# State of a head pair as one block-diagonal matrix, multiplied on the whole TensorE array

## Chip, cores and metric

One core of a Trainium2 chip. The metric is device microseconds (us) of one execution, the median of repeated runs. A span is the time from the first to the last instruction of one profiled execution, which is a little shorter than that execution's own time.

## Reference

Three layers follow each other. B = 2 batches, H = 8 heads, S = 768 positions, D = 64 features per head, so 512 features in all.

```
for t in range(S):                       # retention, gamma differs by head
    state = gamma[None, :, None, None] * state + einsum('bhd,bhe->bhde', k[:, :, t], v[:, :, t])
    y[:, :, t] = scale * einsum('bhd,bhde->bhe', q[:, :, t], state)
x = y.transpose(0, 2, 1, 3).reshape(B, S, 512)

h = (x.transpose(0, 2, 1) @ U @ V)       # U 768x32, V 32x768
u = x + h.transpose(0, 2, 1)
x = u + relu(u @ w_ch1) @ w_ch2          # 512 -> 2048 -> 512

h = relu(x @ w_in)                       # 512 -> 1024
u, v = halves of h
v_n = layer norm of v over its 512 features
v_s = einsum('ts,bsd->btd', w_spatial, v_n) + b_spatial
return (u * v_s) @ w_out                 # 512 -> 512
```

Inputs q, k, v and the biases are 32-bit floats; the weights of U, V, w_ch1, w_ch2, w_in and w_out are 64-bit and are turned into 32-bit on the chip.

## The kernel before

**Retention in chunks.** Heads are taken in pairs, i = 0..7 (four pairs per batch). A pair fills the 128 partitions: head e of the pair has partitions 64e to 64e+63. The 768 positions are cut into six chunks of 128. For each pair the work on TensorE is:

- `scores` (tile `sc`): q times k within each chunk, one matrix of 128x128 for each head and chunk. VectorE, or ScalarE and GpSimd, scale and mask it into `pt` (L418 to L421).
- also in `scores`, L424 to L429 (tile `ds`): what each of the first five chunks adds to the state, k transposed times v, 64x64 for each head. k has been scaled by ScalarE before (`kk`, L395). Then one VectorE scan (L431) runs over the chunks and gives `s`, the state before each of the chunks 1 to 5: 64 features of a head in its own 64 partitions, and along the free axis 64 columns times five chunks, the chunk being the fastest index. So the 64 values of a chunk lie five elements apart.
- `mix` (tile `x`): for each half h of the positions (three chunks), `intra` adds v times `pt` (L450), and `inter` adds state times q for chunks 1 to 5 (L444). The result goes through VectorE into the matrix `X` (L453).
- `turn` (tile `t`, L469) transposes X, `down` (tile `g`) multiplies by U, `up` (tile `hu`) by V.

**Shapes on the array.** The matmuls of these stages use different parts of the 128x128 array, and the plan gives each operation a word for it: "keys" for `scores` (64 rows, 128 columns), "tokens" for `ds` and `intra` (128 rows, 64 columns), "state" for `inter` (64 rows, 64 columns, one head in the upper left quarter and one in the lower right), and False for everything on the whole array: `t`, `g`, `hu` and all later layers. A matmul of 32-bit floats stands as two records (two loads of weights, two matmuls) in the trace; `inter` has 8 pairs x 5 chunks x 2 heads x 2 = 160 of them.

**Order of the work.** No order is written out. Each operation is given to a planner (`Plan`) with a key (roughly a due time), the engines that may do it, a cost in ns, the buffers that it reads and writes, and its word for the array. `arrange` walks forward in modelled time and always gives out the operation that can start first on its engine, by key among those that can start at once. On TensorE an operation whose word differs from that of the one before it is held to start 130 ns later (`span`, L133). `latest` walks backward for the latest end that each operation may have, and `settle` repeats both, ROUNDS times, moving each key towards that latest time by the share BLEND. So the order on all engines, over the whole kernel, comes from the planner's costs, from ROUNDS and from BLEND. Where the planner sees TensorE empty for over 500 ns in the first 60 us, it fills in matmuls whose result nobody reads (tile `idle`). Where an operation may run on VectorE or GpSimd, the planner chooses.

**Buffers.** Pool "a" has 36 slots of 128 x 768 floats and holds q, k, kk, v, `pt`, transposed X and the operands of the later layers. Pool "s" has two slots and holds `s`. A slot is free again when the planner's last reader has ended. All big loads are issued from SyncE.

**After retention.** The channel layer (`c`, `acc`, and `q...`, products in the manner of Strassen) starts on batch 0 while the last pairs of batch 1 are still in retention; then come the gate layer, the spatial product (`pz`) and the output product (`o`). The channel layer's `acc` alone is 768 matmuls of 128x128 by 384 columns.

Of the kernel before, what the change touches and what calls it, by code (L numbers as in the profile page):

```python
# [8 lines left out]
F32 = mybir.dt.float32  # L9
# [12 lines left out]
P = 128  # L22
# [21 lines left out]
class Plan:  # L44
# [16 lines left out]
    def op(self, eng, fn, r=(), w=(), key=None, size=0):  # L61

        o = Op()
        o.key, o.eng, o.fn, o.size = (self.key if key is None else key), dict(eng), fn, size
        deps, bufs = {}, []
        for tok in list(r) + list(w):
            b = tok if isinstance(tok, Buf) else tok[0]
            if isinstance(b, Buf) and b not in bufs:
                bufs.append(b)
                b.left += 1  # L70
        for tok in r:
            if tok in self.last:
                deps[self.last[tok].seq] = self.last[tok]
        for tok in w:
            for x in self.readers.get(tok, ()):
                deps[x.seq] = x
            if tok in self.last:
                deps[self.last[tok].seq] = self.last[tok]
        for tok in w:
            self.last[tok] = o  # L80
            self.readers[tok] = []
        for tok in r:
            if tok not in w:
                self.readers.setdefault(tok, []).append(o)
        o.deps = list(deps.values())
        o.key = max([o.key] + [x.key + 1e-6 for x in o.deps])
        o.bufs, o.outs, o.need, o.seq = bufs, [], len(o.deps), len(self.ops)
        for d in o.deps:
            d.outs.append(o)
        self.ops.append(o)  # L90
        return o
# [206 lines left out]
BIAS = {'V': 0.0, 'G': 0.0, 'A': -200.0}  # L298
HARM = 10.0
NEAR = 5.0  # L300
ROUNDS, BLEND = 14, 0.5
WARM = 11
FILL = 60000.0
AT0, AT1, CH0, CH1 = 6.0, 28.0, 45.0, 15.0
# [18 lines left out]
def tile_kernel(ctx: ExitStack, tc: tile.TileContext, a, out: bass.AP):  # L323
# [10 lines left out]
    def mm(o, l, r, start, stop):  # L334
        nc.tensor.matmul(o, l, r, start=start, stop=stop, skip_group_check=True)  # L335
# [4 lines left out]
    def dma(dst, src, size, r=(), w=(), key=None, eng="D"):  # L340
        op({eng: (55.0, False)}, lambda e: e.dma_start(dst(), src()), r, w, key, size)

    sc_t = const.tile([P, 2 * H + NP * (NCH - 1)], F32, name="scales")
    ksc, msc = sc_t[:, 0:H], sc_t[:, H:2 * H]
    shared = Buf("a", [P, NP + 2, P], F32, "shared")
    GS, TRI, IDENT = [(shared, p) for p in range(NP)], (shared, NP), (shared, NP + 1)

# [50 lines left out]
    def scores(i):  # L398
        b, p = divmod(i, NP)
        for e in range(2):  # L400
            pt_t[i, e] = Buf("a", [P, NCH, P], F32, f"pt{i}{e}")
        for h in range(2):
            sc = [bank([P, TC, P], f"sc{i}{e}{h}") for e in range(2)]

            def run(_, h=h, sc=sc):
                for c in range(TC):
                    sl = slice((TC * h + c) * P, (TC * h + c + 1) * P)
                    for e in range(2):
                        r = slice(64 * e, 64 * e + 64)
                        mm(sc[e].t[:, c, :], k_t[i].t[r, sl], q_t[i].t[r, sl], True, True)  # L410
            op({"P": (690, "keys")}, run, r=[(k_t[i], h), (q_t[i], h)], w=sc)
            for e in range(2):
                m = msc[:, 2 * p + e:2 * p + e + 1]

                def pt(e=e, h=h):
                    return pt_t[i, e].t[:, TC * h:TC * h + TC, :]
                if (2 * h + e) in VIA[i]:
                    op({"A": (582, False)}, lambda E, pt=pt, x=sc[e], m=m: E.activation(pt(), x.t, AF.Copy, scale=m), r=[sc[e], "sc"], w=[(pt_t[i, e], h)])  # L418
                    op({"G": gss(T)}, lambda E, pt=pt: E.tensor_mul(pt(), pt(), tri()), r=[(pt_t[i, e], h), TRI], w=[(pt_t[i, e], h)])
                else:  # L420
                    op({"V": (611, False)}, lambda E, pt=pt, x=sc[e], m=m: E.scalar_tensor_tensor(pt(), x.t, m, tri(), ALU.mult, ALU.mult), r=[sc[e], "sc", TRI], w=[(pt_t[i, e], h)])  # L421
        ds = bank([P, D, NCH - 1], f"ds{i}")

        def run(_):  # L424
            for c in range(NCH - 1):
                for e in range(2):
                    r = slice(64 * e, 64 * e + 64)
                    mm(ds.t[r, :, c], kk_t[i].t[:, c, r], v_t[i].t[:, c, r], True, True)
        op({"P": (600, "tokens")}, run, r=[(kk_t[i], 0), (kk_t[i], 1), v_t[i]], w=[ds])  # L429
        s_t[i] = s = Buf("s", [P, D * (NCH - 1)], F32, f"s{i}")  # L430
        op({"V": (830, False)}, lambda E: E.tensor_tensor_scan(s.t, decay[p // 2].t[:, p % 2, :], ds.t.rearrange("p d c -> p (d c)"), 0.0, ALU.mult, ALU.add), r=[ds, (decay[p // 2], p % 2)], w=[s])  # L431

    def mix(i):
        b, p = divmod(i, NP)
        for h in range(2):
            x = bank([P, TC, P], f"x{i}{h}")
            cs = range(TC * h, TC * h + TC)
            c0 = max(1, TC * h)

            def inter(_, x=x, cs=cs, c0=c0, h=h):  # L440
                for c in cs[c0 - TC * h:]:
                    for e in range(2):
                        r = slice(64 * e, 64 * e + 64)
                        mm(x.t[r, c - TC * h, :], s_t[i].t[r, :].rearrange("p (d c) -> p d c", c=NCH - 1)[:, :, c - 1], q_t[i].t[r, c * P:(c + 1) * P], False, True)  # L444

            def intra(_, x=x, cs=cs, h=h):
                for c in cs:
                    for e in range(2):
                        r = slice(64 * e, 64 * e + 64)
                        mm(x.t[r, c - TC * h, :], v_t[i].t[:, c, r], pt_t[i, e].t[:, c, :], c == cs[0], False)  # L450
            op({"P": (656, "tokens")}, intra, r=[v_t[i], (pt_t[i, 0], h), (pt_t[i, 1], h)], w=[x])
            op({"P": (440 if h == 0 else 655, "state")}, inter, r=[s_t[i], (q_t[i], h)], w=[x])
            op({"V": vps(T)}, lambda E, x=x, h=h: E.tensor_mul(xs(b, p, h).rearrange("p (c t) -> p c t", t=P), x.t, gs(p).unsqueeze(1).to_broadcast([P, TC, P])), r=[x, GS[p]], w=[("X", b, p, h)])  # L453

    def cpy(e, o, i):
# [262 lines left out]
    A = {}  # L718
# [133 lines left out]
    with tc.manual_schedule():  # L852
# [8 lines left out]
            op({"P": (n * 320.0, False)}, lambda _: spend(n), w=[idle])  # L861

        plan.key = -200.0
        dma(lambda: sc_t[:], lambda: a["sc"], P * 36 * 4, w=["sc"], eng="E")
        op({"G": (250.0, False)}, lambda e: e.memset(shared.t[:, NP:NP + 2, :], 1.0), w=[TRI, IDENT])
        for z, (tok, test) in enumerate(((TRI, ALU.is_ge), (IDENT, ALU.is_equal))):
            op({"G": (400.0, False)}, lambda e, z=z, test=test: e.affine_select(shared.t[:, NP + z, :], shared.t[:, NP + z, :], [[1, P]], test, 0.0, base=0, channel_multiplier=-1), r=[tok], w=[tok])
# [98 lines left out]
def _arrays(q, k, v, moe_U, moe_V, moe_w_ch1, moe_w_ch2, moe2_w_in, moe2_w_spatial, moe2_b_spatial, moe2_w_out):  # L966
    import numpy as np

    def c(x):
        return np.ascontiguousarray(x)  # L970

    def featmaj(x):
        return c(x.transpose(0, 1, 3, 2).reshape(B, NP, P, S))

    def tokmaj(x):
        return c(x.reshape(B, NP, 2, NCH, P, D).transpose(0, 1, 4, 3, 2, 5).reshape(B, NP, P, NCH, P))

    gamma = 1.0 - 2.0 ** (-5.0 - np.arange(H, dtype=np.float64))
    t = np.arange(P, dtype=np.float64)
    scale = 1.0 / np.sqrt(D)  # L980
    gs = np.repeat(gamma[:, None] ** t[None, :] * scale, D, axis=0).reshape(NP, P, P)
    ksc = gamma[None, :] ** (P - t[:, None])
    msc = gamma[None, :] ** -t[:, None]
    gc = np.repeat(gamma ** P, D).reshape(NP, P).T
    gc = np.concatenate([np.zeros((P, NP, 1)), np.repeat(gc[:, :, None], NCH - 2, axis=2)], axis=2).reshape(P, NP * (NCH - 1))

    def f32(x):
        return c(x.astype(np.float32))

    def raw(x):  # L990
        return c(x).view(np.uint64)

    def ftiles(x):
        n = x.shape[1] // P
        return raw(x.reshape(ND, P, n, P).transpose(2, 1, 0, 3).reshape(n, P, DM))

    def halves(x):
        return raw(x.reshape(2, 2, P, 2, 2 * P).transpose(1, 3, 2, 0, 4).reshape(ND, P, DM))

    return {  # L1000
        "qT": featmaj(q), "kT": featmaj(k), "k": tokmaj(k), "v": tokmaj(v),
        "gs": f32(gs.transpose(1, 0, 2)), "sc": f32(np.concatenate([ksc, msc, gc], axis=1)),
        "U": raw(moe_U.reshape(NCH, P, R).transpose(1, 0, 2).reshape(P, NCH * R)), "V": raw(np.tile(moe_V, (4, 1)).reshape(P, 2, T).transpose(1, 0, 2)),
        "w1": ftiles(moe_w_ch1),
        "w2": raw(moe_w_ch2.reshape(NF, P, DM)),
        "wu": ftiles(moe2_w_in[:, :DM]), "wv": halves(moe2_w_in[:, DM:]),
        "ws": f32(moe2_w_spatial.T.reshape(NCH, P, S)),
        "bsp": c(moe2_b_spatial.reshape(1, S)),
        "wo": raw(moe2_w_out.reshape(ND, P, DM)),
    }  # L1010
# [17 lines left out]
```

## Time and profile before

| | |
|---|---|
| median of 3 runs | 464.26 us (464.25 to 464.81) |
| the profiled execution: own time | 464.74 us |
| its span | 463.0 us |
| TensorE busy | 457.6 us (99% of the span) |
| VectorE / ScalarE / GpSimd busy | 383.5 / 254.0 / 100.7 us |
| granted TensorE clock | 0.999 of full speed |

The span is 1.7 us shorter than the profiled execution's own time, and that execution is 0.5 us above the median. "Busy" of TensorE counts a matmul from its start to its modelled end, so neighbouring matmuls overlap; the distance from one start to the next says what a matmul costs. Retention runs from about 6 us to about 66 us, from 57 us on mixed with the channel layer, and the rest up to the end is the later layers.

### The profile page before, as it was taken

How to read it: one execution, taken by the hardware profiler on the slowest of the kernel's cores; microseconds unless marked ns; L12 is line 12 of the kernel's file. 1: busy time of each engine (PE TensorE's matmuls, PEld its weight loads, DVE VectorE, ACT ScalarE, POOL GpSimd, SP SyncE). 2: the span in 40 equal slices, each digit the busy share in tenths (PEclk: the TensorE clock that was granted, in tenths of full speed). 3: DMA queues.
4: the chain of work that ended last, by engine and by line, in shares of the span. 5: the costliest groups of instructions: out<-in, count | busy, mean ns of one | idle time of the engine just before them, and what ended most of it. 6: DMA issues, size and time to landing. Idle time of an engine off the chain costs nothing.

```text
span 463.0 us, 8188 instructions
## 1 busy us (share of the span) xinstructions
PE 457.6 (99%) x3150; PEld 442.3 (96%) x3150; DVE 383.5 (83%) x800; ACT 254.0 (55%) x516; POOL 100.7 (22%) x96
## 2 busy tenths in 40 slices
PE   8999999999999999999999999999999999999996
PEld 5898899999999999999999999999999999999885
DVE  2969999999999999999788788899988999965000
ACT  2667676375566665565454445567558698321221
POOL 3165333433313231331131012201310001300000
PEclk9999999999999999999999999999999999999999
DMA  8996313141423324224121112000022032000222
GB/s 303 401 398 239 92 45 92 42 142 50 134 92 91 95 90 136 94 88 138 45 92 46 47 45 69 1 1 9 10 64 91 1 108 76 2 0 1 91 91 92
DMA packets 14583, 43.34 MB, mean 94 GB/s; under 512 B 1744, under 2 KB 2128, under 8 KB 14544
## 3 DMA queue, kind: packets, MB, share of 16 engines
q1 hardware_dynamic: 14400, 42.80, 26.9%
q8 instruction: 25, 0.41, 0.4%
q14 instruction: 14, 0.11, 0.1%
q10 hardware_dynamic: 144, 0.02, 0.0%
HBM read 39.67 MB, written 3.15 MB: 92 GB/s over the span
## 4 chain that ended last, share of the span: by engine, by line
PE 98%; DMA 1%; DVE 0%; ACT 0%; issue 0%; SPq 0%
PE acc L335 29%; PE pz L335 11%; PE c L335 7%; PE o L335 7%; PE x L335 5%; PE sc L335 3%; PE g L335 1%; PE t L469 1%; PE ds L335 1%; DMA k<-in_kT 1%; PE hu L335 1%; PE qu11d L335 0%; PE qu11c L335 0%; PE q40a L335 0%; PE qu11a L335 0%; PE qu01d L335 0%
## 5 line engine op out<-in xcount | busy, mean ns | idle before, releaser
L335 PE MATMUL acc<-a,hw 128*128 128x384 f32 x512 | 130.3, 334 | 0.0
L335 PEld LDWEIGHTS acc<-a,hw 128*128 128x128 f32 x512 | 92.5, 188 | 0.4 <-DVE a L732 0.4
L335 PE MATMUL acc<-a,lw 128*128 128x384 f32 x256 | 85.5, 334 | 0.0
L757 DVE TENSOR_TENSOR x<-acc,x 128x384 f32<-128x384 f32 x128 | 69.4, 548 | 7.1 <-PE acc L335 6.9
L564 POOL TENSOR_TENSOR rw<-rw,tw 128x512 int32<-128x512 int32 x32 | 44.0, 1375 | 112.6 <-DVE rw L563 102.0
L335 PEld LDWEIGHTS acc<-a,lw 128*128 128x128 f32 x256 | 48.0, 188 | 0.0
L730 ACT ACTIVATE y<-y 128x384 f32<-128x384 f32 x36 | 18.9, 525 | 39.3 <-DVE y L729 39.2
L560 ACT ACTIVATE yw<-raww 128x512 f32<-128x512 f32 x32 | 21.6, 676 | 16.7 <-DVE rw L563 16.4
L563 DVE SCALAR_TENSOR_TENSOR rw<-yw,rw 128x512 uint32<-128x512 uint32 x32 | 24.1, 757 | 0.0
L732 DVE TENSOR_TENSOR a<-y,a 128x384 fp32r<-128x384 f32 x36 | 21.0, 584 | 2.7 <-ACT a L731 2.4
L561 ACT ACTIVATE tw<-raww 128x512 int32<-128x512 uint32 x32 | 21.5, 673 | 2.0 <-POOL rw L564 2.0
L456 ACT COPY out<-o 128x512 f32<-128x512 f32 x12 | 7.1, 589 | 24.4 <-PE o L335 24.4
L731 ACT CAST a<-y 128x384 fp32r<-128x384 f32 x36 | 18.5, 514 | 1.1
L335 PE MATMUL pz<-ws,vn 128*128 128x384 f32 x108 | 19.0, 334 | 0.0
L335 PE MATMUL pz<-hws,vn 128*128 128x384 f32 x72 | 18.9, 334 | 0.0
L421 DVE SCALAR_TENSOR_TENSOR pt<-sc,scales,shared 128x384 f32<-128x384 f32 x21 | 11.9, 609 | 8.4 <-PE sc L335 8.3
L335 PEld LDWEIGHTS pz<-ws,vn 128*128 128x128 f32 x108 | 18.8, 188 | 0.0
L562 DVE TENSOR_SCALAR rw<-yw 128x512 uint32<-128x512 uint32 x32 | 18.2, 580 | 0.1
L573 DVE TENSOR_TENSOR lw<-rw,hw 128x512 fp32r<-128x512 f32 x20 | 17.1, 853 | 0.0
L335 PE MATMUL c<-f00b,hw 128*128 128x384 f32 x64 | 16.4, 337 | 0.0
L335 PE MATMUL c<-f01b,hw 128*128 128x384 f32 x64 | 16.2, 334 | 0.0
L572 ACT CAST hw<-rw 128x512 fp32r<-128x512 f32 x20 | 12.4, 618 | 6.3 <-POOL rw L564 5.9
(886 smaller groups left out, 1222.8 us busy)
## 6 DMA issues: line engine op xcount, KB each, us to landing
raww<-in_w SPq DMA_DIRECT2D x32, 512.0 KB, 3.6
q<-in_qT SPq DMA_DIRECT2D x8, 384.0 KB, 8.1
k<-in_kT SPq DMA_DIRECT2D x8, 384.0 KB, 8.1
kk<-in_k SPq DMA_DIRECT2D x8, 384.0 KB, 7.9
v<-in_v SPq DMA_DIRECT2D x8, 384.0 KB, 8.2
out_y<-out SPq DMA_DIRECT2D x12, 256.0 KB, 2.0
raws<-in_ws SPq DMA_DIRECT2D x6, 384.0 KB, 2.9
rawwu<-in_wu SPq DMA_DIRECT2D x4, 512.0 KB, 3.8
```

The source lines that it names most:

```text
L335: nc.tensor.matmul(o, l, r, start=start, stop=stop, skip_group_check=True)
L560: op({"A": c}, lambda E: E.activation(y.t, words(1).bitcast(F32), AF.Copy, scale=2.0 ** -112), r=whole, w=[y])
L561: op({"A": c}, lambda E: E.activation(t.t, words(0), AF.Copy, scale=2.0 ** -29), r=whole, w=[t])
L562: op({"V": vone(n)}, lambda E: E.tensor_single_scalar(r.t, y.t.bitcast(U32), 3, ALU.logical_shift_left), r=[y], w=[r])
L563: op({"V": vss(n)}, lambda E: E.scalar_tensor_tensor(r.t, y.t.bitcast(U32), 0x80000000, r.t, ALU.bitwise_and, ALU.bitwise_or), r=[y, r], w ...
L564: op({"G": gss(n)}, lambda E: E.tensor_tensor(r.t.bitcast(I32), r.t.bitcast(I32), t.t, ALU.add), r=[r, t], w=[r])
L572: op({"A": acp(DM)}, lambda E: E.copy(h.t, f(r.t)), r=[r], w=[h])
L573: op({"V": vss(DM), "G": gss(DM)}, lambda E: E.tensor_sub(l.t, f(r.t), f(h.t)), r=[r, h], w=[l])
L730: op({"A": (525, False)}, lambda E: E.activation(y[0](), y[0](), AF.Relu), r=[y[1]], w=[y[1]])
L731: op({"A": acp(T)}, lambda E: E.copy(t.t[:, 0, :], y[0]()), r=[y[1]], w=[(t, 0)])
L732: op({"V": vss(T), "G": gss(T)}, lambda E: E.tensor_sub(t.t[:, 1, :], y[0](), f(t.t[:, 0, :])), r=[y[1], (t, 0)], w=[(t, 1)])
L757: op({"V": vps(T)}, lambda E, o=o, v=xs(b, d, h): E.tensor_add(v, o.t, v), r=[o, ("X", b, d, h)], w=[("X", b, d, h)])
```

## The change

`s` stays as it is, the scan's output in pool "s". Behind it, ScalarE copies it twice into a new tile `bd` of pool "a": 128 partitions x 5 chunks x 2 x 64 columns. Copy e writes the 64 columns of head e for all five chunks and multiplies each partition by `own_rows[:, e]`, which is 1 in the partitions of head e and 0 in the others. So `bd` holds for each chunk a 128x128 matrix with the state of head 0 in the upper left block, that of head 1 in the lower right, and zeros elsewhere; its columns lie next to each other. `own_rows` comes with the table of scales, which grows from 36 to 38 columns.

`inter` then takes one matmul of 128x128 by 128 columns for a chunk in place of two of 64x64 by 128, and its word for the array is False in place of "state". It waits for both copies in place of the scan. The planner's settings ROUNDS and BLEND change too.

```diff
-ROUNDS, BLEND = 14, 0.5
+ROUNDS, BLEND = 20, 0.4
...
-    sc_t = const.tile([P, 2 * H + NP * (NCH - 1)], F32, name="scales")
-    ksc, msc = sc_t[:, 0:H], sc_t[:, H:2 * H]
+    sc_t = const.tile([P, 2 * H + NP * (NCH - 1) + 2], F32, name="scales")
+    ksc, msc, own_rows = sc_t[:, 0:H], sc_t[:, H:2 * H], sc_t[:, 2 * H + NP * (NCH - 1):]
...
-        s_t[i] = s = Buf("s", [P, D * (NCH - 1)], F32, f"s{i}")
+        s = Buf("s", [P, D * (NCH - 1)], F32, f"s{i}")
         op({"V": (830, False)}, lambda E: E.tensor_tensor_scan(s.t, decay[p // 2].t[:, p % 2, :], ds.t.rearrange("p d c -> p (d c)"), 0.0, ALU.mult, ALU.add), r=[ds, (decay[p // 2], p % 2)], w=[s])
+        s_t[i] = bd = Buf("a", [P, NCH - 1, 2, D], F32, f"bd{i}")
+        for e in range(2):
+            op({"A": (470, False)}, lambda E, e=e: E.activation(bd.t[:, :, e, :], s.t.rearrange("p (d c) -> p c d", c=NCH - 1), AF.Copy, scale=own_rows[:, e:e + 1]), r=[s, "sc"], w=[(bd, e)])
...
                 for c in cs[c0 - TC * h:]:
-                    for e in range(2):
-                        r = slice(64 * e, 64 * e + 64)
-                        mm(x.t[r, c - TC * h, :], s_t[i].t[r, :].rearrange("p (d c) -> p d c", c=NCH - 1)[:, :, c - 1], q_t[i].t[r, c * P:(c + 1) * P], False, True)
+                    mm(x.t[:, c - TC * h, :], s_t[i].t[:, c - 1, :, :].rearrange("p e d -> p (e d)"), q_t[i].t[:, c * P:(c + 1) * P], False, True)
...
-            op({"P": (440 if h == 0 else 655, "state")}, inter, r=[s_t[i], (q_t[i], h)], w=[x])
+            op({"P": (440 if h == 0 else 655, False)}, inter, r=[(s_t[i], 0), (s_t[i], 1), (q_t[i], h)], w=[x])
...
-        dma(lambda: sc_t[:], lambda: a["sc"], P * 36 * 4, w=["sc"], eng="E")
+        dma(lambda: sc_t[:], lambda: a["sc"], P * 38 * 4, w=["sc"], eng="E")
...
-        "gs": f32(gs.transpose(1, 0, 2)), "sc": f32(np.concatenate([ksc, msc, gc], axis=1)),
+        "gs": f32(gs.transpose(1, 0, 2)), "sc": f32(np.concatenate([ksc, msc, gc, np.repeat(np.eye(2), D, axis=0)], axis=1)),
```

## Rows read from the trace of the kernel before

**Rows 1.** The page, part 1: busy time, share, instructions of each engine.

```profile
PE 457.6 (99%) x3150; PEld 442.3 (96%) x3150; DVE 383.5 (83%) x800; ACT 254.0 (55%) x516; POOL 100.7 (22%) x96
```

**Rows 2.** Waits of PE, whole span: releaser, us in total, times, longest.

```profile
PE idle L335 <- PEq L1017: 0.8, 1, 0.8
PE sc L335 <- DMA k<-in_kT: 0.6, 1, 0.6
PE t L469 <- DVE x L453: 0.3, 1, 0.3
```

**Rows 3.** Busy time by engine in two stretches; last three: clock, DMA share, GB/s.

```profile
8.00:66.00 58.00, 57.72 (x807) 51.68 (x806) 50.16 (x98) 38.18 (x81) 23.24 (x24) 1.00 0.66 251
...
66.00:200.00 134.00, 133.97 (x776) 133.65 (x776) 131.66 (x250) 79.39 (x151) 43.18 (x34) 1.00 0.32 99
```

**Rows 4.** Timeline of PE, 10 to 25 us: start, length, work, shape, records.

```profile
10.57 1.40 PE L335 MATMUL x<-q,s 64*64 64x128 f32 x20
11.90 1.61 PE L335 MATMUL sc<-q,k 64*128 64x128 f32 x24
...
14.88 1.48 PE L335 MATMUL x<-pt,v 128*64 128x128 f32 x24
16.31 1.41 PE L335 MATMUL x<-q,s 64*64 64x128 f32 x20
17.65 1.61 PE L335 MATMUL sc<-q,k 64*128 64x128 f32 x24
19.19 0.87 PE L469 MATMUL t<-shared,x 128*128 128x128 f32 x6
19.99 0.80 PE L335 MATMUL ds<-v,kk 128*64 128x64 f32 x20
...
22.12 1.40 PE L335 MATMUL x<-q,s 64*64 64x128 f32 x20
23.45 1.69 PE L335 MATMUL g<-xtok,ust 128*128 128x256 f32 x12
24.99 0.49 PE L469 MATMUL t<-shared,x 128*128 128x128 f32 x3
```

**Rows 5.** Timeline of PE around 48 us: a double group of state products.

```profile
47.98 2.55 PE L335 MATMUL x<-q,s 64*64 64x128 f32 x40
50.46 1.76 PE L469 MATMUL t<-shared,x 128*128 128x128 f32 x12
```

**Rows 6.** Timeline of PE, 62 to 70 us: the last state products, in the channel layer.

```profile
62.47 0.51 PE L335 MATMUL c<-f01b,hw 128*128 128x384 f32 x2
62.82 0.34 PE L335 MATMUL c<-f01b,lw 128*128 128x384 f32 x1
63.09 1.41 PE L335 MATMUL x<-q,s 64*64 64x128 f32 x20
64.47 0.55 PE L469 MATMUL t<-shared,x 128*128 128x128 f32 x3
...
67.75 1.59 PE L335 MATMUL g<-xtok,ust 128*128 128x256 f32 x12
69.18 0.51 PE L335 MATMUL c<-f00b,hw 128*128 128x384 f32 x2
```

**Rows 7.** Weight loads by shape, 8 to 66 us: busy us, mean ns, idle before.

```profile
L335 PEld LDWEIGHTS x<-q,s 64*64 64x64 f32 x160 | 9.7, 194 | 1.3 <-issue 0.8 <-DVE s L431 0.4
...
L335 PEld LDWEIGHTS g<-xtok,ust 128*128 128x128 f32 x36 | 4.5, 190 | 0.3
```

**Rows 8.** Timeline of DVE, 9 to 24 us: the first two scans.

```profile
9.44 0.82 DVE L431 TENSOR_TENSOR_SCAN s<-decay,ds 128x320 f32<-128x320 f32 x1 [0.77 <-PE ds L335]
...
15.45 0.81 DVE L431 TENSOR_TENSOR_SCAN s<-decay,ds 128x320 f32<-128x320 f32 x1
```

**Rows 9.** Groups of ACT, 8 to 66 us: busy us, mean ns, idle before.

```profile
L395 ACT ACTIVATE kk<-kk,scales 128x384 f32<-128x384 f32 x15 | 8.6, 616 | 5.9 <-DMA kk<-in_k 5.9
...
L526 ACT CAST f00b<-x 128x384 fp32r<-128x384 f32 x8 | 3.7, 514 | 1.9 <-DVE x L497 1.9
```

## Prediction

> **What bounds the kernel now.** I read the page first: TensorE is busy for 457.6 of 463.0 us, the others far less [rows 1]. A full TensorE alone doesn't prove that it sets the time, so the waits come next: over the whole span its matmuls wait 1.7 us in all, 0.8 and 0.6 of it before the first result is possible, and 0.3 near the end of retention [rows 2]. Behind that nothing stops it. So whatever is saved on TensorE's own list of work shortens the kernel, as long as the other engines deliver as early as they are then asked to, and each wait that a new order brings is added in full. The busy times by stretch show who might not: in 8 to 66 us, where the change acts, ScalarE works 38.2 of 58 us and VectorE 50.2; from 66 to 200 us VectorE works 131.7 of 134 us [rows 3]. Last I read TensorE's timeline through retention, start to start, because there the price of a matmul and of a change of shape can be separated.
>
> **State products, the stream itself.** A group of 40 records takes 47.98 to 50.46, 2.48 us [rows 5]; one of 20 takes 1.34 us (16.31 to 17.65; 1.33 at 10.57 and 22.12) [rows 4]. The 20 further records cost 1.14 us. A chunk's product has four records, two per head, and the heads' records run side by side, so that is ten steps of 0.114 us: two steps to a chunk, 80 in the kernel. What is left of a group of 20, 1.34 - 1.14 = 0.20 us, is paid once per group, for going into the shape and out of it.
>
> After the change a chunk has two records of 128 columns on the whole array: again 80 steps. No row shows such a 32-bit product. From below the nearest is `sc`: a step loads 128 columns too, streams 128, and a group of 24 records (12 steps) takes 1.54 us [rows 4]; less the same 0.20, 0.112 a step. From above it is `g`, whose loads of 128 columns on the whole array last 190 ns [rows 7] and which in mid-stream takes 1.43 us for 12 (67.75 to 69.18) [rows 6], 0.119 a step. The stream so moves by -0.2 to +0.4 us; I take 0.115, **+0.1 us**. That the array now multiplies by zeros in half of its cells costs nothing by itself: both halves were already busy at the same moment.
>
> Is the wider load hidden behind the matmul before it? In `g` it is: 0.119 us a step holds both a load of 190 ns (a latency) and 256 columns. [...]
>
> **State products, the changes of shape.** There are eight groups of them between 10.57 and 64.47 us, with 20, 20, 20, 8, 20, 12, 40 and 20 records. The words behind them are: `sc`, `sc`, `g`, tokens, `t`, `hu`, `t`, `t`; ahead of them tokens seven times, and `c` once, at the last. Work on the whole array pays on entry as well: a `g` group straight after state products takes 1.54 us (23.45 to 24.99) [rows 4] and one within whole-array work 1.43 [rows 6], so 0.11 us.
> - Behind three groups stand `sc` or tokens: the new form enters for about 0.11 and leaves for what it left for before. I count zero.
> - Behind `g`: before, 0.20 for the state group and 0.11 for entering `g`; after, 0.11 once. Saved: 0.20 us. Behind `hu` and two `t` it is the same trade, but no row isolates their entry: saved is 0.09 (entry free) to 0.20 each, I take 0.15. Together 0.65 us.
> - The last group has whole-array work on both sides, and all its changes go: 63.09 to 64.47 is 1.38 us where ten steps are 1.14, and the `c` record before it takes 0.27 (62.82 to 63.09) where two take 0.35 (62.47 to 62.82) [rows 6]. Saved: 0.24 + 0.09 = 0.33 us, and up to 0.11 for entering `t`; I take 0.38.
> - The planner no longer charges 130 ns between `inter` and whole-array work, so it will put more of them together: of the three other groups I let two meet a `t`, 0.15 each, 0.30 us; bounds 0 and 0.6.
> Sum of these: **-1.33 us**.
>
> **The two copies on ScalarE.** Sixteen operations of 320 elements. Two rows bound one: the scaled `kk` at 616 ns and the plain `f00b` at 514, both for 384 elements [rows 9]; by length 430 (514 x 320/384) to 616. At 0.53 that is 8.5 us more in a stretch where ScalarE has 19.8 us idle [rows 3]. So it doesn't become full (46.7 of 58), and the busy time itself costs nothing: what hides it is ScalarE's idle time. What counts is the delay. State products start right when the scan is done: 15.45 + 0.81 = 16.26 against 16.31, and 10.26 against 10.57 [rows 4, 8]; the loads waited 0.4 us for it [rows 7]. Two copies one after the other, and the hand-over, put about 1.1 us between. In that time TensorE must do something else.
> - First pair: products possible at about 11.4, `intra` done at 10.57: 0.8 us open. The next pair's `sc` (11.90 before) may come first, if its q and k are there; no row says how long they had been. I take half, 0.4 us.
> - Second pair: possible at 17.4, `intra` done at 16.31: 1.1 us open, and the first pair's `t` (0.80 us at 19.19 for the like of it [rows 4]) can stand there. 0.1 to 0.3 us is left, I take 0.1.
> - Later pairs: two or more are in flight, with `g`, `hu`, `t` and the next `sc` (1.54 us) as cover, and in the end the channel layer. Zero; if that cover were missing, up to 1.1 us for each pair.
> Together **+0.5 us**, bounds 0 and 1.9 for these two pairs. Queued behind a copy on ScalarE, which takes its list in order, are `kk` for the next pair's `ds`, the copies out of `t`, and weight conversion; ScalarE waited 5.9 us for data before `kk` [rows 9], so a copy mostly takes an idle place.
>
> **Edits with no price.** Two more columns of scales ride in a load that is needed long after TensorE's first wait; `bd` takes a slot of the 36 for some 3 us while transfers queue anyway; the scan and VectorE's list are unchanged. ROUNDS and BLEND reorder the whole kernel: behind 66 us TensorE waits for nothing, so a new order can't gain there and can only lose. I take zero for it and leave the loss to the rivals.
>
> **Sum.** +0.1 - 1.33 + 0.5 = -0.73 us. The profiled execution would go from 464.74 to 464.0 us, its span from 463.0 to 462.3. It lies 0.5 above the median; from the median 464.26 it is 463.5 us. Its own range, from the bounds above, is 462.5 to 464.6. A measurement of this kernel tells a difference from none at about 0.2%, 0.93 us, so the forecast lies at the border: within that case I give two parts in five to faster by more.
>
> **Rivals.**
> 1. *The planner gains more.* With the fourth shape gone, groups of `inter` join `t`, `hu` and `c` on both sides, as the last group does for 0.33 us or more, and the early delays are covered. Four more groups at 0.33, and no 0.5: 463.5 - 1.3 - 0.5 = 461.7 us. For it: each state group still pays its 0.20 us today. Against: tokens must come before every `inter` of the same pair.
> 2. *Slower: the copies come late.* ScalarE's order puts other work ahead of them, and TensorE stands before `inter`. Each pair has 1.1 us to hide; with five of eight open by 0.5 us beyond what I charge, 463.5 + 2.5 = 466.0. It ends slower than before from 0.7 us of further waits on. For it: the margin behind the scans of 0.05 and 0.3 us. Against: 19.8 us idle on ScalarE, other work on TensorE from the third pair on.
> 3. *Hidden: VectorE sets the pace behind 66 us.* It has 2.3 us of idle time in 134 [rows 3]. If it can't deliver 0.7 us earlier, TensorE gets ahead and waits: 464.2, within 0.2%. Against: TensorE has never waited for it there, so its list holds work done ahead of need, and GpSimd, which may take part of it, is idle for 91 of those 134 us.
> 4. *The wide loads aren't hidden.* Each of 80 steps then stands 0.11 us longer, the entry that `g` pays: +8.8 us, 472.2 us. [...] `g` speaks against it.
>
> **Chances.** Forecast 0.49 (0.20 faster by over 0.2%, 0.29 within); rival 1 0.27 (faster); rival 2 0.15 (slower); rival 3 0.06 (0.04 within, 0.02 slower); rival 4 0.03 (slower). So faster 0.47, same 0.33, slower 0.20. The range 461.2 to 465.6 takes in the forecast, most of rival 1 and the milder part of rival 2, and leaves out about 0.2.
>
> **What the new profile would show.** 80 records `x<-q,bd` of 128*128 in place of 160, with 0.112 to 0.119 us from start to start. Fewer changes of shape in TensorE's timeline: no extra 0.1 us between `inter` and a `t`, `hu` or `g` beside it. Sixteen copies at 0.43 to 0.62 us, ScalarE at about 47 us in 8 to 66. Between 10 and 18 us a wait or some `idle` matmuls before `inter`. TensorE's waits behind 66 us still near zero. The prediction is wrong if steps cost 0.2 us or more, if `inter` waits for ScalarE by more than 1 us in sum, or if the new order leaves TensorE waiting in the later layers.

## The result, and the profile after

The changed kernel takes 468.17 us, the median of five runs (467.99 to 468.5); the kernel before takes 464.25. The ratio is 1.0082, between 1.0070 and 1.0094: 3.9 us slower, where 0.7 us faster was forecast. The profiled execution took 468.5 us, its span is 466.8 us against 463.0.

TensorE is nearly as full as before (98% against 99%), by the page's line of busy times:

```profile
PE 459.3 (98%) x3072; PEld 442.6 (95%) x3072; DVE 373.5 (80%) x791; ACT 265.1 (57%) x532; POOL 110.1 (24%) x105
```

The stretches of [rows 3] show where it isn't (us; busy time of PE, PEld, DVE, ACT, POOL; clock, DMA share, GB/s):

```profile
8.00:66.00 58.00, 55.42 (x693) 48.18 (x692) 44.18 (x87) 47.92 (x95) 28.68 (x29) 1.00 0.68 259
66.00:200.00 134.00, 134.00 (x799) 133.75 (x796) 127.82 (x250) 80.25 (x151) 43.68 (x36) 1.00 0.27 91
```

In 8 to 66 us TensorE does nothing for 2.6 us, before for 0.3. From 66 to 200 us it never stops, and VectorE, which was to become the bound in rival 3, has more room than before (127.8 of 134). The waits of TensorE name who is late:

```profile
PE x L335 <- ACT bd L434: 1.9, 2, 1.0
PE idle L335 <- PEq L1018: 0.8, 1, 0.8
PE hu L335 <- DVE gt L489: 0.6, 1, 0.6
PE qv10c L335 <- DVE yv L670: 0.3, 1, 0.3
```

The tile `bd` (ns: shortest, median, longest) shows the product as forecast and the copies not:

```profile
L335 PEld LDWEIGHTS x<-q,bd x80: 186/192/192, 12.0 to 72.7; 128*128 128x128 f32 x80
L335 PE MATMUL x<-q,bd x80: 272/275/377, 12.0 to 72.8; 128*128 128x128 f32 x80
L434 ACT ACTIVATE bd<-s,scales x16: 847/890/955, 10.4 to 57.9; 128x320 f32<-128x320 f32 x16
```

A copy lasts 0.89 us where 0.53 was taken and 0.62 was the upper bound. What that does stands in TensorE's timeline (start, length, work, records, the wait before it):

```profile
9.23 1.48 PE L335 MATMUL x<-pt,v 128*64 128x128 f32 x23
10.64 0.50 PE L335 MATMUL idle<-const-bfloat16-1.0 128*128 128x384 bf16 x2
12.03 1.38 PE L335 MATMUL x<-q,bd 128*128 128x128 f32 x10 [0.89 <-ACT bd L434]
...
35.29 0.94 PE L335 MATMUL x<-q,bd 128*128 128x128 f32 x6
36.06 0.49 PE L470 MATMUL t<-shared,x 128*128 128x128 f32 x3
37.53 0.71 PE L335 MATMUL x<-q,bd 128*128 128x128 f32 x4 [0.97 <-ACT bd L434]
...
42.12 1.69 PE L335 MATMUL g<-xtok,ust 128*128 128x256 f32 x12
...
45.54 1.16 PE L335 MATMUL hu<-vst,gt 128*128 128x384 f32 x5 [0.55 <-DVE gt L489]
```

and in ScalarE's beside it:

```profile
10.36 1.62 ACT L434 ACTIVATE bd<-s,scales 128x320 f32<-128x320 f32 x2 [1.81 <-DVE s L431]
...
35.81 1.66 ACT L434 ACTIVATE bd<-s,scales 128x320 f32<-128x320 f32 x2
...
43.09 1.67 ACT L434 ACTIVATE bd<-s,scales 128x320 f32<-128x320 f32 x2 [0.21 <-DVE s L431]
44.66 0.36 ACT L488 CAST gt<-g 128x256 fp32r<-128x256 f32 x1
```

and in VectorE's:

```profile
45.05 0.43 DVE L489 TENSOR_TENSOR gt<-g,gt 32x256 fp32r<-32x256 f32 x1 [1.42 <-ACT gt L488]
```

For the first pair TensorE has nothing real to do from 10.64 to 12.03, 1.39 us (two `idle` matmuls and the wait). At 37.53 it waits for copies that ended at 37.47. At 45.54 the wait is named after VectorE, but VectorE itself waited 1.42 us for ScalarE's `gt`, which stood behind two copies: `g` ended at 43.81 (42.12 + 1.69), and `gt` started at 44.66, as the second copy ran out (44.76). So a long copy delays other work on ScalarE's list too.

### The profile page after: what moved, and what is told of

Its sections match the earlier page's. It is cut to its first block, busy times and chain, and to the rows that moved or that the text cites. A ratio compares the mean times of both kernels' runs of the same rounds, so it can differ in the third digit from the quotient of the medians.

```text
span 466.8 us, 8057 instructions
## 1 busy us (share of the span) xinstructions
PE 459.3 (98%) x3072; PEld 442.6 (95%) x3072; DVE 373.5 (80%) x791; ACT 265.1 (57%) x532; POOL 110.1 (24%) x105
## 4 chain that ended last, share of the span: by engine, by line
PE 92%; ACT 5%; DVE 2%; issue 0%; ACTq 0%; DVEq 0%
PE acc L335 29%; PE pz L335 11%; PE c L335 7%; PE o L335 7%; PE x L335 3%; PE sc L335 2%; ACT bd L434 2%; PE idle L335 1%; PE g L335 1%; PE ds L335 1%; PE t L470 1%; ACT kk L395 1%; PE hu L335 1%; DVE s L431 1%; PE qu11d L335 0%
## 5 line engine op out<-in xcount | busy, mean ns | idle before, releaser
L564 DVE SCALAR_TENSOR_TENSOR rw<-yw,rw 128x512 uint32<-128x512 uint32 x32 | 22.1, 695 | 0.0
L434 ACT ACTIVATE bd<-s,scales 128x320 f32<-128x320 f32 x16 | 13.6, 890 | 4.5 <-DVE s L431 4.5
```

What stands on the lines that cost most here:

```text
L434: op({"A": (470, False)}, lambda E, e=e: E.activation(bd.t[:, :, e, :], s.t.rearrange("p (d c) -> p c d", c=NCH - 1), AF.Copy, scale=own_r ...
L564: op({"V": vss(n)}, lambda E: E.scalar_tensor_tensor(r.t, y.t.bitcast(U32), 0x80000000, r.t, ALU.bitwise_and, ALU.bitwise_or), r=[y, r], w ...
```

## The experiments

Two theories were to be told apart: the copies are late because they are long, or the new order (the planner's settings, and its plan for another set of operations) costs by itself; with a third, that the wide product is dearer than its rows say. Ten of the kernels were planned anew after each edit. Their result was that a new plan moves the time by as much as the edit does. So the last five hold an order fixed, as e3 and e5 had done, and these carry the verdict. The ratio in the table is to the kernel before run beside each, whose median lay between 464.25 and 464.85 us, so the ratios are compared and not the times alone. e1, e2, e5, e12, f1, f3 and f4 came out between or beyond the ranges that had been named for them, and e3 and e7 in the range of a theory, though not for its reason.

| | us | ratio to before (95%) |
|---|---|---|
| after | 468.17 | 1.0082 (1.0070 to 1.0094) |
| **planned anew** | | |
| e1 after, settings 14, 0.5 | 471.1 | 1.0143 (1.0128 to 1.0158) |
| e2 before, settings 20, 0.4 | 465.96 | 1.0028 (1.0017 to 1.0040) |
| e4 copies made, not read | 466.67 | 1.0047 (1.0033 to 1.0062) |
| e12 the same, 14, 0.5 | 473.41 | 1.0196 (1.0172 to 1.0221) |
| e8 no copies | 464.87 | 1.0010 (1.0000 to 1.0019) |
| e11 the same, 14, 0.5 | 466.92 | 1.0054 (1.0037 to 1.0071) |
| e6 planner told 850 ns a copy | 469.87 | 1.0117 (1.0102 to 1.0132) |
| e7 copies on VectorE | 472.08 | 1.0162 (1.0147 to 1.0178) |
| e9 state by steps | 469.61 | 1.0112 (1.0097 to 1.0127) |
| e10 the same, BLEND 0.25 | 467.69 | 1.0071 (1.0056 to 1.0086) |
| **order kept** | | |
| e3 after's, flat copies, strided loads | 472.61 | 1.0175 (1.0160 to 1.0191) |
| e5 after's, copies read in order | 466.75 | 1.0054 (1.0037 to 1.0071) |
| f1 after's, copies not issued | 464.73 | 1.0011 (1.0001 to 1.0020) |
| f2 after's, short copies | 464.89 | 1.0015 (1.0005 to 1.0024) |
| f5 after's, short copies, both awaited | 465.53 | 1.0017 (1.0007 to 1.0027) |
| f4 after's, old products, no copies | 466.05 | 1.0039 (1.0024 to 1.0054) |
| f3 before's, new products, no copies | 463.93 | 0.9995 (0.9986 to 1.0005) |

**e1, e2: the settings.**

```diff
-ROUNDS, BLEND = 20, 0.4
+ROUNDS, BLEND = 14, 0.5
```

(e1 in the changed kernel; e2 the reverse in the kernel before.)

> The changed kernel with ROUNDS and BLEND as before (14, 0.5). If the copies are what costs (theory A: a pair of them takes 1.65 us where the planner was told 0.94, so products with the state start late), it stays well above the kernel before, 466 to 469 us, whatever the order. If the new order is what costs (theory B: 20 rounds at 0.4 plan worse for this work), it comes down to 463.5 to 464.3 us.

> The kernel before with ROUNDS and BLEND 20, 0.4 and nothing else. Theory A: within 0.3% of before, 463.5 to 465.5 us, with TensorE waiting for under 2 us. Theory B: 466.5 us or more.

Each form is faster at its own settings: the old one by 1.7 us, the new one by 2.9. So the loss isn't in the new settings as such: with the old ones the changed kernel is slower still. But a change of settings isn't free either.

**e3, e5: the strides.** In after's order on every engine. The copy of after reads 64 values that lie 20 bytes apart for each chunk. e3 writes them in the order in which they are read, and the product's weight load then skips; e5 reads in order and writes 512 bytes apart.

```diff
e3
+bd = Buf("a", [P, 2, D, NCH - 1], F32, f"bd{i}")
+  E.activation(bd.t[:, e, :, :].rearrange("p d c -> p (d c)"), s.t, AF.Copy, scale=...)
+  mm(..., s_t[i].t.rearrange("p e d c -> p (e d) c")[:, :, c - 1], ...)
e5
+  E.activation(bd.t[:, :, e, :].rearrange("p c d -> p d c"), s.t.rearrange("p (d c) -> p d c", c=NCH - 1), ...)
```

> The changed kernel with the blocks kept in the scan's own order: bd is head, feature, chunk, so each copy reads and writes 320 neighbouring elements, and TensorE picks every fifth column when it loads. The order of the work is the same on every engine. Theory A with the reading stride as the reason that a copy takes 0.85 to 0.89 us: copies of 0.45 to 0.5 us, the waits of TensorE on them shrink from 1.9 us to under 0.5, time 465 to 466.5 us; what is planned as idle stays. Theory that the length of a copy doesn't matter, only its place in ScalarE's list: 467.5 us or more. If the scaling by a column is what is dear in a copy, copies stay above 0.55 us.

> The changed kernel, same order of work on all engines, same layout of bd; only the copies walk the other way: they read 320 neighbouring elements and write them 512 bytes apart. The run with flat copies showed 0.56 us a copy but 0.222 us a product where columns lie five apart, against 0.112 where they are neighbours. If the reading stride makes the copy slow: copies 0.55 to 0.6 us, products 0.112, time 462.5 to 464.5 us (the 472.6 of the flat copies less 80 x 0.11). If any stride does, on either side: copies of 0.85 us or more, time within 0.3% of the changed kernel's 468.2. If the place of a copy in the list counts and not its length: 467 or more with short copies.

The tile `bd` of e3:

```profile
L335 PEld LDWEIGHTS x<-q,bd x80: 295/317/321, 10.7 to 76.5; 128*128 128x128 f32 x80
L335 PE MATMUL x<-q,bd x80: 322/386/488, 10.7 to 76.6; 128*128 128x128 f32 x80
L434 ACT ACTIVATE bd<-s,scales x16: 545/562/572, 9.6 to 59.3; 128x320 f32<-128x320 f32 x16
```

The same 320 elements take 0.56 us instead of 0.89 once both sides are contiguous. The stride has moved to TensorE, where it costs far more: loads of 317 instead of 192 ns, no longer hidden: each of the first group's ten records costs 0.10 us more (2.33 us to the next work against 1.36). In e5, with the stride on the writing side, a copy lasts 0.86 us by median, and the first pair is shorter. Its line in the tile view, and ScalarE's timeline:

```profile
L434 ACT ACTIVATE bd<-s,scales x16: 795/864/891, 9.8 to 56.1; 128x320 f32<-128x320 f32 x16
```

```profile
9.76 1.45 ACT L434 ACTIVATE bd<-s,scales 128x320 f32<-128x320 f32 x2 [1.81 <-DVE s L431]
```

Pairs of copies that stand back to back last 1.45 to 1.52 us instead of 1.62 to 1.74, and the ratio falls by 0.28% (1.0082 to 1.0054, 1.3 us). The two traces bear 1.2 us of that out: e5's span is 1.8 us shorter, but 0.6 of this lies ahead of the first copy, where both have the same list (the first `x<-pt` starts at 8.52 us against 9.12).

**e4, e8, e11, e12: no copies in the product's way.** The product takes 128 neighbouring columns of `s`, so its values aren't the state; in e4 and e12 the copies are still made.

```diff
+  mm(x.t[:, c - TC * h, :], s_t[i].t[:, 48 * (c - 1):48 * (c - 1) + P], ...)   # waits for the scan
-  for e in range(2): op({"A": (470, False)}, ... bd ...)                      # e8 and e11 only
```

> The products on the whole array take their 128 columns straight from the scan's result (other numbers, no zeros), and wait for the scan alone; the two copies per pair are still made, but nobody reads them. This leaves out the block structure. Theory A (delay): the delay is gone and the shapes saved remain, 462.8 to 464.2 us. If ScalarE's load itself is what costs (13.6 us more in retention): 466 us or more.

> As the earlier run with products that take their 128 columns straight from the scan's result and wait for it alone, and now the copies are left out too (so no block structure; other numbers). This is the change of shapes alone, at settings 20, 0.4, to be set against 465.96 us, the kernel before at these settings. Theory that the shapes save 1.3 us: 464.2 to 465.2 us. Theory that they save nothing that the order doesn't give back: 465.7 to 466.7. Against the run with unread copies, 466.67, it tells what the copies' load alone costs on ScalarE: 1 to 2 us if it does.

> Products on the whole array straight from the scan's result, no copies (no block structure, other numbers), at settings 14, 0.5: the second reading of what the shapes alone save, against 464.3 us, the kernel before at these settings. If the 1.1 us found at 20, 0.4 is the shapes: 462.8 to 463.6 us. If it was the luck of an order: anything from 464 to 467.

> The same with the copies made and not read, at settings 14, 0.5: the second reading of the copies' load on ScalarE. At 20, 0.4 the load cost 1.8 us and the waiting for copies another 1.5. If load and waiting cost alike here: 464.5 to 466.5 us, leaving 4 to 6 us of the changed kernel's 471.1 to the waiting and the order. If the load is harmless: within 0.5 us of the run without copies.

Copies that nobody reads cost 1.8 us at one setting and 6.5 at the other. In e12 most of it is two new waits, by TensorE's waits:

```profile
PE hu L335 <- DVE gt L489: 4.5, 2, 2.3
```

One of them, 2.17 us before `hu` at 59.97, has ScalarE's `gt` (58.68) behind a pair of copies and a weight conversion, like the wait of 45.54 us above; the other, 2.31 us at 88.42, stands far behind the last copy (58.23). So the plans of e11 and e12 differ in more than the copies, and these four settle neither a size nor that ScalarE's queue is the reason.

**e6, e7: tell the planner, or use another engine.**

```diff
-op({"A": (470, False)}, ... E.activation ...)
+op({"A": (850, False)}, ... E.activation ...)            # e6
+op({"V": (480, True)}, ... E.tensor_scalar_mul ...)      # e7
```

> The changed kernel with the planner told 850 ns for a copy in place of 470; settings 20, 0.4. If the loss comes from planning with too low a cost, the planner pulls other work ahead of the products: waits of TensorE on the copies under 0.5 us, 464 to 466.5 us. If the delay can't be covered by other work whatever the planner knows: 467 to 470 us, with planned idle in place of waits.

> The changed kernel with both copies on VectorE, right behind the scan (480 ns told). If the delay between scan and products is what costs: copies of 0.4 to 0.5 us, no change of engine, 463.5 to 466 us, unless VectorE, 44 of 58 us busy in retention, becomes late. If VectorE pays for the reading stride as ScalarE does: copies of 0.8 us or more and 467 us or more.

Both are slower than after. On VectorE a copy with the same 20-byte stride is short, and the kernel as planned anew around it is still slower than after; where it loses wasn't followed up:

```profile
L434 DVE TENSOR_SCALAR bd<-s,scales x16: 548/569/1432, 9.7 to 70.4; 128x320 f32<-128x320 f32 x16
```

**e9, e10: the state without a stride.** The scan becomes a copy and four dependent steps, chunk after chunk, so that `s` and `bd` both have runs of 64 neighbours. The planner is told 560 ns for a copy, and the tables of decays are gone, so here too more than one thing changes.

```diff
-E.tensor_tensor_scan(s.t, decay..., ds..., 0.0, ALU.mult, ALU.add)
+E.tensor_copy(s.t[:, 0:D], ds.t[:, 0, :])
+for c in range(1, NCH - 1):
+    E.scalar_tensor_tensor(s.t[:, c * D:(c + 1) * D], s.t[:, (c - 1) * D:c * D], decay(p), ds.t[:, c, :], ALU.mult, ALU.add)
```

> The changed kernel with the scan replaced by five short VectorE operations, one for each chunk, so that the state lies chunk by chunk, and the copies on ScalarE read and write runs of 64 neighbours (560 ns told; the tables of decays for the scan are gone). Settings 20, 0.4. If stride on either side makes the copy slow: copies of 0.45 to 0.6 us. If their length is what costs: 464.5 to 466.5 us, between the run without copies (464.87) and the changed kernel (468.17). If the hand-over to ScalarE and its load cost whatever the length: 467 us or more. Should the five operations take more than 1.2 us together, VectorE's part is what shows.

> The run before with BLEND 0.25: another order for the same work. If the order decides as much as the work does, it differs from the run at 0.4 by 1 us or more, and it may fall below the kernel before (463 to 465.5). If the work decides, the two agree within 0.7 us.

In e9 the copies are short, and the steps give part of it back: 0.22 + 4 x 0.28 = 1.34 us in place of a scan of 0.82.

```profile
L429 DVE COPY s<-ds x8: 210/216/226, 8.9 to 56.0; 128x64 f32<-128x64 f32 x8
L431 DVE SCALAR_TENSOR_TENSOR s<-s,scales,ds x32: 280/281/282, 9.2 to 57.2; 128x64 f32<-128x64 f32 x32
L435 ACT ACTIVATE bd<-s,scales x16: 545/560/565, 10.4 to 58.0; 128x320 f32<-128x320 f32 x16
```

BLEND alone moves this form by 1.9 us. e10 is the fastest kernel here with the whole computation and the new product other than e5, and both stay slower than before.

**f1 to f4: one thing at a time in a kept order.** f1 leaves the copies in the plan and doesn't issue them; f2 issues them contiguous on both sides; f4 is f1 with the two products of before; f3 is the kernel before, in its own order, with the wide product on `s`. The values of the state are changed in f1, f2 and f3.

```diff
f1 (from after)
-  E.activation(bd.t[:, :, e, :], ...)
+  None
+  mm(..., raw_s[i].t[:, 48 * (c - 1):48 * (c - 1) + P], ...)
f2 (from after)
+  E.activation(bd.t.rearrange("p c e d -> p (c e d)")[:, 320 * e:320 * e + 320], s.t, AF.Copy, ...)
```

> The changed kernel's plan, and so its order on every engine, but the sixteen copies aren't issued; the products on the whole array take 128 columns straight from the scan's result and wait for the scan (no block structure, other numbers). What this is below 468.2 us is what the copies cost at a fixed order: load, delay and waits. If the copies are the cause of the loss: 462.5 to 464.5 us, a drop of 4 us or more. If the order is: 466.5 us or more.

> The changed kernel in its own order, with copies that read and write 320 neighbours (0.56 us, as the flat copies were) and products that load 128 neighbouring columns of what was written (other numbers, no block structure). Load, hand-over and waits stay, only the copies are 0.3 us shorter each. If the strides of the copy are what costs: 463.5 to 465 us (472.6 of the flat copies less 80 x 0.11 us for their strided loads = 463.8). If it is the step to ScalarE as such: 466.5 us or more.

> The kernel before in its own order, with one product of 128x128 in place of two of 64x64 for each chunk, its 128 columns taken straight from the scan's result (other numbers). The shape alone, nothing else moved. The prediction's terms give 0.65 + 0.38 less 0.1, so 463.2 to 463.6 us. If an earlier TensorE only waits for others: 464.1 to 464.5.

> The kernel before's work (two products of 64x64 per chunk, no copies, waiting for the scan) in the changed kernel's order. The order alone. If the new order is as good as the old for this work: 464 to 465 us. If the order is what costs, with idle slots planned in it: 466.5 us or more. Less the run with copies not issued, it is the shape's worth in the new order.

Without copies after's order takes 464.73, with short ones 464.89. But in f2 the first matrix lies within the first copy, so its product starts at 10.36 us, before the second copy is done. f5 mends that.

**f5: both copies awaited.**

```diff
f5 (from f2)
+  mm(..., s_t[i].t.rearrange("p c e d -> p (c e d)")[:, 180 + 20 * c:180 + 20 * c + P], ...)
```

> The run with short copies again, with one difference: each product's 128 columns lie across the border of the two copies, so every product waits for both, as in the changed kernel (in the run before, the products of the first two chunks read only what the first copy had written). Other numbers, no block structure. If the length of the copies is what costs: within 0.7 us of the 464.9 of that run. If it was the earlier start after the first copy: 466 us or more.

It differs from after in the copies' strides and in which 128 neighbouring columns are read: ratio 1.0017 against 1.0082. The products themselves cost the same in both (loads of 192 ns, ten records in 1.38 us). The copies in the tile view, TensorE's wait for them in sum, and its timeline at the places shown of after:

```profile
L434 ACT ACTIVATE bd<-s,scales x16: 546/564/586, 10.4 to 54.7; 128x320 f32<-128x320 f32 x16
PE x L335 <- ACT bd L434: 0.5, 2, 0.3
```

```profile
10.72 0.50 PE L335 MATMUL idle<-const-bfloat16-1.0 128*128 128x384 bf16 x2
11.51 1.38 PE L335 MATMUL x<-q,bd 128*128 128x128 f32 x10 [0.28 <-ACT bd L434]
...
34.33 0.94 PE L335 MATMUL x<-q,bd 128*128 128x128 f32 x6
35.10 0.49 PE L470 MATMUL t<-shared,x 128*128 128x128 f32 x3
35.77 0.71 PE L335 MATMUL x<-q,bd 128*128 128x128 f32 x4 [0.18 <-ACT bd L434]
...
42.83 1.43 PE L335 MATMUL hu<-vst,gt 128*128 128x384 f32 x6
```

Both kernels do the same work in the same order, so their starts can be laid side by side. Up to the first copy they run level (the first `x<-pt` at 9.12 us in after, 9.21 in f5). At the first product after is 0.52 us later (12.03 against 11.51), at the group of six 0.96 (35.29 against 34.33), at the next four 1.76 (37.53 against 35.77). The wait for `gt` doesn't exist in f5. At `x` of the last pair after is 2.84 us later (72.27 against 69.43), and the span ends 2.9 us later (466.8 against 463.9): all of it is lost before the last state products, and none is given back.

## Why the prediction was wrong

At kept orders the difference comes apart into four parts, each the step from one ratio to the next:

| from | to | what changes | ratio |
|---|---|---|---|
| before | f3 | the product's shape | 1 to 0.9995, -0.05% |
| f3 | f1 | the order | to 1.0011, +0.16%, 0.7 us |
| f1 | f5 | short copies, hand-over, waits for them | to 1.0017, +0.06%, 0.3 us |
| f5 | after | the copies' strides | to 1.0082, +0.65%, 3.0 us |

By the ratios the first three are near what measurement can tell, the fourth is far above it. The traces agree on the fourth. Where TensorE starts its first `x<-pt` differs from one execution to another by up to 0.8 us with the same list up to there (8.38 us in e3, 9.21 in f5), so they are compared from that start to the end of the span: 454.0 us in before, 453.2 in f3, 453.9 in f1, 454.7 in f5, 457.6 in after. The four steps are then -0.7, +0.6, +0.9 and +2.9 us.

- **The stream itself: right.** Groups of 10 and of 4 records last 1.38 and 0.71 us; six records so cost 0.67, 0.112 a step, where 0.112 to 0.119 was the forecast. The loads last 192 ns and are hidden in these steps. Rival 4 is out: its steps would have been 0.11 longer, and `g`, which the prediction set against it, was the right row to go by. Loads that skip (e3, 317 ns) aren't hidden: 0.10 us more a record.
- **Changes of shape: right in one order, too large in the other, at the `t`s.** In after's order the old products cost 1.32 us more than the new ones (f4 466.05, f1 464.73), where the sum of this step and the stream was 1.23. That they agree is partly luck: after's order has eleven groups of state products, and the sum counted before's eight. In before's order it is 0.36 by the medians, and the interval reaches from a gain of 0.65 to a loss of 0.2; by the traces it is 0.7. f3's timeline says which term failed:

```profile
21.47 1.38 PE L335 MATMUL x<-q,s 128*128 128x128 f32 x10
22.61 1.68 PE L335 MATMUL g<-xtok,ust 128*128 128x256 f32 x12
...
31.83 1.38 PE L335 MATMUL x<-q,s 128*128 128x128 f32 x10
33.05 1.38 PE L469 MATMUL t<-shared,x 128*128 128x128 f32 x9
34.36 1.61 PE L335 MATMUL sc<-q,k 64*128 64x128 f32 x24
...
61.63 0.33 PE L335 MATMUL c<-f01b,lw 128*128 128x384 f32 x1
61.80 1.28 PE L335 MATMUL x<-q,s 128*128 128x128 f32 x10
63.14 0.33 PE L469 MATMUL t<-shared,x 128*128 128x128 f32 x1
```

  The middle group in the kernel before:

```profile
32.71 1.40 PE L335 MATMUL x<-q,s 64*64 64x128 f32 x20
34.04 1.29 PE L469 MATMUL t<-shared,x 128*128 128x128 f32 x9
35.26 1.61 PE L335 MATMUL sc<-q,k 64*128 64x128 f32 x24
```

  The group ahead of `g` takes 1.14 us where it took 1.33 [rows 4]: 0.19 saved, as forecast. Where a `t` follows, almost nothing is: the middle group and its nine `t` records take 2.53 us (31.83 to 34.36) and took 2.55 (32.71 to 35.26), where 0.15 was taken. The last group, between whole-array work on both sides, takes 1.34 where it took 1.38 [rows 6]: 0.04, not 0.24. Only the `c` ahead of it gave its 0.10 (0.17 in place of 0.27). So a `t` behind state products costs about as much when they fill the whole array; why, no run says.
- **The two copies on ScalarE: this step failed, at the length of a copy.** 0.53 us was taken, between 0.43 and 0.62; 0.89 was measured, so a pair of copies stands 1.62 to 1.74 us between scan and product, not 1.1. The prediction's own sign of being wrong, `inter` waiting for ScalarE by more than 1 us in sum, was met: 1.9 us in after, against 0.5 in f5. The rows it was taken from [rows 9] read and write neighbours; the copy reads every fifth value, which stood in the diff. f5, with no stride, measures 0.56: as a price for neighbours the bounds held. For these 320 elements the time moved with the distance: read 20 bytes apart 0.89 us (after), written 512 bytes apart 0.86 (e5), 4 bytes apart on both sides 0.56 (e3, f5). The prediction priced the copy by its number of elements alone. For VectorE these runs don't test the distance: its copy read 20 bytes apart lasts 0.57 us (e7), and none without a stride was run beside it.
- **First pair: short even at the right length.** 0.8 us was seen as open and half of it taken, in the hope that the next `sc` would come first. The planner didn't put it there: f5 has 0.79 us (10.72 to 11.51), 0.34 of it the two `idle` matmuls that f1 has in the same place without any copy (10.63 to 10.97); after has 1.39. The second pair cost nothing: `sc` stands ahead of it and the product follows at 19.65 without a wait, where 0.1 was taken.
- **Later pairs, zero: failed.** 0.97 us at 37.53, and 0.55 at 45.54 behind `gt`. The first is the case named with the zero (cover gone, "up to 1.1 us"). The second was not seen: ScalarE's other clients were named, but as taking idle places. That the copies fill only idle time (47.9 of 58, forecast 46.7) was true and didn't help.
- **ROUNDS and BLEND, zero: off by 0.7 us.** The prediction let a new order lose only behind 66 us, and took zero. With the new products it loses just there: from the first `x<-pt` to the last `acc`, f1 and f3 take the same 312.45 us, f1's two `idle` matmuls included, and f1 loses 0.6 us behind it. Most of that is one place in the gate layer, where `qv10c` waits for VectorE's `yv`. That wait stands in every trace in after's order, among the waits of after shown above too, and in neither before nor f3. f1's timeline:

```profile
364.97 0.28 PE L335 MATMUL qv11a<-hwv1a,f11b 128*128 128x256 f32 x1
365.59 0.98 PE L335 MATMUL qv10c<-qwv,f11t 128*128 128x256 f32 x6 [0.34 <-DVE yv L670]
```

  0.62 us lie between two starts where the records ahead follow each other every 0.12. With the old products after's order loses in retention as well: f4 has 44 changes of shape on TensorE between 8 and 85 us, where before has 34, and it is 0.9 us behind before at the last `acc`. With the new products the fourth word is gone and the orders are closer, 32 in f1 and 28 in f3.
- **The rivals and the range.** Rival 2 is what happened in its effect, priced at 466.0 us, measured at 468.2. Its reason, other work ahead of the copies, shows in part: at 35.81 they start 0.50 us behind the end of the scan (35.31), in f5 0.10; mostly it is their length. Rival 1 wasn't reached: even without copies e8 needs 464.87. Rival 3 isn't seen. The range of the sum was added up too narrowly: the bounds of its terms give 462.2 to 465.8 us and not 462.5 to 464.6, and the measured time lies outside either.

From f5 to e5 to after, at one order, the first pair of copies takes 1.01, 1.45 and 1.62 us and the ratio is 1.0017, 1.0054 and 1.0082. So 0.44 us more for a pair costs 1.7 us in the kernel and 0.61 costs 3.0, four to five times as much, with eight pairs; the traces, from the first `x<-pt` on, give 1.7 and 2.9. Not settled: which part of the 0.65% is the product's wait and which the others on ScalarE's queue (of 2.9 us between the two traces 0.5, 0.8 and 0.6 stand at the three waits shown, the rest in smaller delays between), and whether a plan exists in which the new form wins. f3 leaves out the blocks of zeros and so isn't such a kernel.

## What to carry to other kernels

Before costing a copy, write down the byte distance between neighbouring elements on both its sides, and price it by a row with that distance, not by one with the same length alone: here ScalarE took 0.89 us for 320 elements at 20 bytes and 0.56 at 4. An operation put between a producer and a full engine cost its latency here wherever the plan had no cover (waits of 0.89 and 0.97 us in after), and delayed what queued behind it (0.55 us at `hu`), though its own engine, ScalarE, was idle for a sixth of the time. Where a planner reorders everything, compare at a kept order first: here the same work planned anew came out 1.7 to 6.7 us apart. And compare two traces from a place that the change can't have moved, since here their starts alone differ by up to 0.8 us.

## What the hardware showed unexpectedly

- Reading 320 floats 20 bytes apart, ScalarE needs 0.89 us instead of 0.56; VectorE does the same copy in 0.57 (e7); what it needs without the stride wasn't run.
- A weight load of 128 columns lying 20 bytes apart takes 317 instead of 192 ns, and is no longer hidden: a group of ten records takes 2.33 us to the next work (10.68 to 13.01 in e3) against 1.36 in after (12.03 to 13.39). The old products read at the same distance, 64 columns a load, with loads of 194 ns by mean [rows 7], and cost 0.114 a step [rows 5]. The loads start two at a time there (two at 16.31 us in before, done in 0.19); whether it is this or the 64 columns that makes the difference, no run tests.

```profile
10.68 2.49 PE L335 MATMUL x<-q,bd 128*128 128x128 f32 x10 [0.28 <-ACT bd L434]
13.01 0.49 PE L470 MATMUL t<-shared,x 128*128 128x128 f32 x3
```
